# A decay table built from a tile already loaded, and a small load issued later

## The chip, the cores and the metric

One core of a Trainium2 chip. The metric is the device time of one execution in microseconds; the kernel before takes 591.12 us (median of 3 runs, 590.98 to 591.58). Engines: TensorE (PE; PEld is its weight load), VectorE (DVE), ScalarE (ACT), GpSimd (POOL) and SyncE (SP). Each of SP and ACT can issue DMAs on a queue of its own: in this profile q1 carries what SP issues, q10 what ACT issues. The work of all queues is done by the core's 16 DMA engines.

## The reference

Three stages, all in float32. First a decayed linear attention over 2 batches, 8 heads, 768 positions and head size 64:

```
for each block b of 64 positions:
    intra = (q_b k_b^T * Dmask) v_b          # Dmask[h,i,j] = lam[h]^(i-j) for i >= j, else 0
    inter = (q_b * lam[h]^(i+1)) kv_state
    out_b = intra + inter
    kv_state = lam[h]^64 * kv_state + (k_b * lam[h]^(63-i))^T v_b
```

`lam` has 8 values, one per head. The result, as 1536 tokens of 512, goes through a gated feed-forward layer (`w_gate`, `w_val`, `w_out`, width 1536), and its result through a layer of 8 experts (width 1024): a router (`moe2_w_gate`, 512 x 8) picks one expert for each token, and the expert's output is scaled by the router's probability.

## The kernel before, in words

The attention works on 12 units: 6 chunks of 128 positions, 2 batches each, all 8 heads at once as 4 pairs. A unit loads three tiles `in0`, `in1`, `in2` (q, k, v) of 128 x 512; `load(u)` (line 227) issues them on SP, and five units are asked for at the start. Only unit 0's k is loaded in two halves. Then `em_T` (line 285) transposes q and k on PE (line 295), ACT copies the results (line 297), and POOL makes `kd`, the decayed k (line 304). `em_S` (line 307) computes the scores on PE (line 315) and DVE multiplies them by the table `dec` (line 318). `em_O` (line 325) multiplies kd by v for the state (line 332), the state by the decayed q from the second chunk on (line 343), and the masked scores by v (line 347); ACT and DVE split the result into a rounded part and a rest (lines 353 and 356), `x1`. DVE keeps the state (lines 361 and 363).

Each engine runs its instructions in the order in which the program emits them; waits between engines are set by the tiles they read and write. In the first units the order is: transposes of unit u+1, then `em_O` of u, then scores of u+1.

Two tables are built at the start. `dec` (powers of lam, lower triangle, line 260) comes from `lam_b`, which holds the 8 values of lam in each of the 128 partitions (one load on ACT's queue, line 238). `lrep` (line 269) holds, in partition x*64+d, pair p, position i, the power i+1 of lam of head 2p+x; it is a running product on DVE over a scratch tile `d2`, whose first half holds the factors and whose second half holds the start values. `lrep` is read for the decayed q (line 301) and for the decay of the state (line 335), both from the second chunk on. Its factors come from `lam_s`, where partitions 0 to 63 hold the even heads' values and 64 to 127 the odd heads': two loads on ACT's queue (line 240), each with 64 partitions x 4 values taken with a stride of two. The scratch tiles `d0`, `d1`, `d2` are three of the four buffers tagged `raw`.

`wr`, the router's weights, is loaded on ACT's queue at line 248 and first read by `parts3` at line 574, in the second pass (t = 1) of the gate stage.

After the attention, `em_GV` (line 445) multiplies x1 by the gate and value weights in 36 groups of 24 matmuls (`mm3`, line 204), each product as three matmuls of rounded parts and rests. Weights come through the `raw` ring on SP's queue (`pump_dma`, line 102); ACT rounds a piece (line 141, `bg_begin`) and DVE computes the rest (line 149, `bg`). Some of these steps already run in the attention's last units. The matmuls of the output weights, the routing and the experts follow.

Of the kernel before, what the change touches and what calls it, by code (L numbers as in the profile page):

```python
# [8 lines left out]
F32 = mybir.dt.float32  # L9
# [11 lines left out]
def decayed_attention_two_moes(  # L21
# [14 lines left out]
    nc = tc.nc  # L36
    B, H, S, D = q.shape
# [3 lines left out]
    P = 128  # L41
    NP = H // 2
# [17 lines left out]
    const = ctx.enter_context(tc.tile_pool(name="const", bufs=1))  # L60
# [41 lines left out]
    def pump_dma():  # L102
        n = at["dma"]
        if n < len(pieces):
            src = pieces[n][2]
            pool, tag = ring.pop(0)
            ring.append((pool, tag))
            r = pool.tile([P, 1024], U32, tag=tag, name=tag)
            dst = (r if src.dtype == U32 else r.bitcast(F32))[:, 0:src.shape[1] * src.shape[2]]
            nc.sync.dma_start(out=dst.rearrange("p (a b) -> p a b", a=src.shape[1]), in_=src)  # L110
            raws[n] = r
            at["dma"] = n + 1
# [9 lines left out]
    def bg_begin():  # L122

        i = at["split"]
        if i >= len(pieces):
            return
        key, j, _src = pieces[i]
        if key not in W and not free:
            return
        if not (wide and i < N1):  # L130
            if i in raws:
                fin.append(raws.pop(i).bitcast(F32)[:, 0:512 if i < N1 else 1024])
        if not fin:
            return
        if key not in W:
            slot_of[key] = pool, s = free.pop(0)
            W[key] = pool.tile([P, 2048], F32R, tag=f"w{s}", name=f"w{s}")
        x = fin.pop(0)
        w = W[key][:, j * 1024:(j + 1) * 1024] if i < N1 else W[key]
        n = w.shape[1] // 2  # L140
        nc.scalar.copy(out=w[:, 0:n], in_=x)  # L141
        lop.append((i, w[:, n:2 * n], x, w[:, 0:n].bitcast(F32)))
        at["split"] = i + 1

    def bg(stage):
        if stage == 0:
            if lop:
                _i, lo, x, hi = lop.pop()
                nc.vector.tensor_tensor(out=lo, in0=x, in1=hi, op=ALU.subtract)  # L149
                pump_dma()  # L150
            if mid and not fin:
                a, r = mid.pop()
                nc.vector.tensor_scalar(out=a, in0=a, scalar1=2.25, scalar2=None, op0=ALU.max)
                cur.append((a, r))
        elif stage == 1:
            if cur:
                a, r = cur[0]
                u = a.bitcast(U32)
                nc.vector.tensor_scalar(out=u, in0=u, scalar1=3, scalar2=None, op0=ALU.logical_shift_left)
                nc.vector.scalar_tensor_tensor(out=u, in0=r[:, :, 1], scalar=0x80000000, in1=u,  # L160
                                               op0=ALU.bitwise_and, op1=ALU.bitwise_or)
            i = at["abs"]
            if wide and i < N1 and not mid and i in raws:
                r = raws.pop(i).rearrange("p (f w) -> p f w", w=2)
                a = cvp.tile([P, 512], F32, tag="cv", name="cv")
                nc.scalar.activation(out=a, in_=r[:, :, 1].bitcast(F32), func=ACTF.Abs, scale=65536.0)
                mid.append((a, r))
                at["abs"] = i + 1
        else:
            if cur:  # L170
                a, r = cur.pop()
                u = a.bitcast(U32)
                nc.vector.scalar_tensor_tensor(out=u, in0=r[:, :, 0], scalar=29, in1=u,
                                               op0=ALU.logical_shift_right, op1=ALU.bitwise_or)
                fin.append(a)
# [34 lines left out]
    nc.vector.memset(warm, 0.0)  # L210
    nc.scalar.activation(out=warm, in_=warm, func=ACTF.Tanh)
    lam_b = const.tile([P, H], F32, name="lam_b")
    lam_s = const.tile([P, NP], F32, name="lam_s")
    wr = const.tile([P, KD, E], F32, name="wr")

    rp = ctx.enter_context(tc.tile_pool(name="rp", bufs=2))
# [10 lines left out]
    def load(u):  # L227
        c, b = units[u]
        for n, src in enumerate((q, k, v)):
            t = ap.tile([P, H, D], F32, tag=f"in{n}", name=f"in{n}", bufs=5)  # L230
            w = H // 2 if u == 0 and n == 1 else H
            for h in range(0, H, w):
                nc.sync.dma_start(out=t[:, h:h + w, :],
                                  in_=src[b, h:h + w, c * P:(c + 1) * P, :].rearrange("h s d -> s h d"))
            qkv[u, n] = t

    load(0)
    nc.scalar.dma_start(out=lam_b, in_=lam.unsqueeze(0).to_broadcast([P, H]))
    for x in range(2):
        nc.scalar.dma_start(  # L240
            out=lam_s[x * D:(x + 1) * D, :],
            in_=lam.rearrange("(p x) -> x p", x=2)[x:x + 1, :].to_broadcast([D, NP]),
        )
    load(1)
    load(2)
    load(3)
    load(4)
    nc.scalar.dma_start(out=wr, in_=w_router.rearrange("(k p) e -> p k e", p=P))


    dec = ap.tile([P, 2, NP, P], F32, name="dec")
# [5 lines left out]
    for x in range(2):  # L257
# [3 lines left out]
        out=dec.rearrange(flat), data0=d0.rearrange(flat), data1=d1.rearrange(flat),  # L261
        initial=0.0, op0=ALU.mult, op1=ALU.add,
    )
    d2 = rawp.tile([P, 2, NP, P], F32, tag="raw", name="raw")
    nc.vector.memset(d2[:, 1], 0.0)
    nc.vector.tensor_copy(out=d2[:, 1, :, 0:1], in_=lam_s.unsqueeze(2))
    nc.vector.tensor_copy(out=d2[:, 0], in_=lam_s.unsqueeze(2).to_broadcast([P, NP, P]))
    nc.vector.memset(d2[:, 0, :, 0:1], 0.0)
    nc.vector.tensor_tensor_scan(
        out=lrep.rearrange("j p i -> j (p i)"),  # L270
# [14 lines left out]
    def em_T(u):  # L285
        c, b = units[u]
        for n in range(2):
            pt = bank(cnt["t"] % 2).rearrange("p (a b) -> p a b", a=NP)
            cnt["t"] += 1
            t = ap.tile([P, NP, P], F32, tag=f"tT{n}", name=f"tT{n}", bufs=2)  # L290
            w = NP // 2 if u == 0 and n == 1 else NP
            for p in range(NP):
                if p == w:
                    pt = bank(7).rearrange("p (a b) -> p a b", a=NP)
                nc.tensor.transpose(pt[:, p, :], pair(qkv[u, n], p), ident)  # L295
                if p % w == w - 1:
                    nc.scalar.copy(out=t[:, p + 1 - w:p + 1, :], in_=pt[:, p + 1 - w:p + 1, :])
            (qT, kT)[n][u] = t
            if n == 0 and c > 0:
                qd[u] = ap.tile([P, NP, P], F32, tag="qd", name="qd", bufs=3)  # L300
                nc.vector.tensor_tensor(out=qd[u], in0=t, in1=lrep, op=ALU.mult)
        if c < NCH - 1:
            kd[u] = ap.tile([P, H, D], F32, tag="kd", name="kd", bufs=2)
            nc.gpsimd.tensor_tensor(out=kd[u].rearrange("s (p x) d -> s p x d", x=2),
                                    in0=qkv[u, 1].rearrange("s (p x) d -> s p x d", x=2), in1=rev, op=ALU.mult)

    def em_S(u, conv):
        pss = []
        for x in range(2):
            pss.append(bank(2 + cnt["s"] % 3).rearrange("p (a b) -> p a b", a=NP))  # L310
            cnt["s"] += 1
        for p in range(NP):
            for x in range(2):
                r = slice(x * D, (x + 1) * D)
                nc.tensor.matmul(pss[x][:, p, :], lhsT=kT[u][r, p, :], rhs=qT[u][r, p, :], start=True, stop=True)  # L315
        for x in range(2):
            t = ap.tile([P, NP, P], F32, tag=f"at{x}", name=f"at{x}", bufs=2)
            nc.vector.tensor_tensor(out=t, in0=pss[x], in1=dec[:, x], op=ALU.mult)
            att_w[u, x] = t
            if conv:  # L320
                bg(1 + x)
        qT.pop(u)
        kT.pop(u)
# [49 lines left out]
    for u in range(NU):  # L373
        conv = u >= 4 and u % 2 == 1
        if conv:
            bg_begin()
        if u < AHEAD:
            em_T(u + 1)
            em_O(u, conv)
            em_S(u + 1, conv)  # L380
        else:
            if u == AHEAD:
                em_T(u + 1)
            if u + 2 < NU:
                em_T(u + 2)
            if u + 1 < NU:
                em_S(u + 1, conv)
            elif conv:
                bg(1)
                bg(2)  # L390
            em_O(u, conv)
        if u + 5 < NU:
            load(u + 5)
        if u in (2, 4):
            pump_dma()
            pump_dma()
    att.close()


# [452 lines left out]
    for n in range(len(seq) + LAG):  # L852
        bg(0)
        bg_begin()
        if n < len(seq):
            e, f = seq[n]
# [11 lines left out]
        if n >= LAG:  # L868
            e, f = seq[n - LAG]
# [125 lines left out]
```

## Time and profile before

| | |
|---|---|
| median of the runs (range) | 591.12 us (590.98 to 591.58) |
| profiled execution | 590.82 us |
| its span, from first to last record | 589.0 us |
| busy: PE, DVE, ACT, POOL | 561.8, 392.5, 241.6, 102.9 us |
| chain that ended last | PE 77%; issue 10%; DMA 5%; DVE 4%; POOL 2%; ACT 1% |
| packets on q1, q10 | 78128, 2768 |
| mean granted clock of PE | 0.992 |

The page also cuts the span into 40 slices of 14.7 us, with the busy share of each in tenths, 9 being 90% or more, PEclk being the granted clock:

```profile
PE   4999999999999999999999999989999999999991
PEclk9999999999999999999999999999999999999996
DMA  7999132322220322220122176327697677660000
```

The first slice and the last are the ones in which PE is far from full. Times in all views count from the start of the span; what lies between the span and the time of the execution is 590.82 - 589.0 = 1.8 us.

### The profile page before, as it was taken

The numbers are of one execution on the slowest core, as the hardware profiler recorded it, in microseconds if no ns is written. First come the engines' busy times: TensorE is split into PE (matmuls) and PEld (weight loads), VectorE is DVE, ScalarE is ACT, GpSimd is POOL, SyncE is SP. The second block draws the span as 40 slices with busy tenths as digits, with TensorE's granted clock in tenths as the row PEclk, the third lists the DMA queues.
The fourth block names the chain that finished last, engine by engine and source line by source line (L and its number), as shares of the span: only waits on it lengthen the run. The fifth ranks groups of instructions, "written<-read, shape, count | busy, mean of one in ns | idle before, by whom it ended". The sixth has DMA issues, their size and how long they took to land.

```text
span 589.0 us, 8506 instructions
## 1 busy us (share of the span) xinstructions
PE 561.8 (95%) x3202; PEld 465.6 (79%) x3202; DVE 392.5 (67%) x778; ACT 241.6 (41%) x434; POOL 102.9 (17%) x102
## 2 busy tenths in 40 slices
PE   4999999999999999999999999989999999999991
PEld 3888888888888888888888888678888888888881
DVE  4577799888414888562586467886868887777530
ACT  2343244443332444300343333234767666666420
POOL 3325200000000000000000013313265245142001
PEclk9999999999999999999999999999999999999996
DMA  7999132322220322220122176327697677660000
GB/s 130 203 242 215 38 108 107 108 92 88 74 69 0 108 85 95 71 72 0 35 75 101 41 251 195 112 106 232 156 303 247 207 264 238 198 204 28 0 25 31
DMA packets 84011, 72.97 MB, mean 124 GB/s; under 512 B 43228, under 2 KB 69852, under 8 KB 83968
## 3 DMA queue, kind: packets, MB, share of 16 engines
q1 hardware_dynamic: 78128, 65.02, 37.1%
q0 software_dynamic: 3072, 7.35, 3.7%
q8 instruction: 26, 0.43, 0.3%
q10 hardware_dynamic: 2768, 0.03, 0.3%
q14 instruction: 17, 0.14, 0.1%
HBM read 66.09 MB, written 7.08 MB: 124 GB/s over the span
## 4 chain that ended last, share of the span: by engine, by line
PE 77%; issue 10%; DMA 5%; DVE 4%; POOL 2%; ACT 1%; SPq 0%; POOLq 0%; ACTq 0%; DVEq 0%
PE b L204 58%; PE b L629 6%; PE b L630 3%; DMA in<-in_q_dram 2%; PE b L347 2%; PE b L332 2%; PE b L315 1%; PE b L295 1%; PE b L343 1%; DMA gg<-gd,g_idx 1%; POOL out_dram L674 1%; POOL xg L594 1%; PE b L512 1%; DMA xg<-x2d,g_first 1%; DMA in<-in_k_dram 1%
## 5 line engine op out<-in xcount | busy, mean ns | idle before, releaser
L204 PE MATMUL b<-x,w 128*128 128x512 f32 x864 | 199.6, 394 | 0.0
L204 PEld LDWEIGHTS b<-x,w 128*128 128x128 f32 x864 | 162.7, 188 | 36.3 <-issue 0.2
L204 PE MATMUL b<-w,hT 128*128 128x512 f32 x432 | 105.0, 398 | 0.0
L204 PE MATMUL b<-w,h 128*128 128x512 f32 (+1 forms) x384 | 101.0, 398 | 0.0
L204 PEld LDWEIGHTS b<-w,hT 128*128 128x128 f32 x432 | 79.9, 188 | 18.2
L629 PE MATMUL b<-xT,w 128*128 128x480 f32 x224 | 77.0, 383 | 0.1
L204 PEld LDWEIGHTS b<-w,h 128*128 128x128 f32 (+1 forms) x384 | 65.1, 183 | 14.7 <-ACT h L636 0.4
L630 PE MATMUL b<-xT,w 128*128 128x240 f32 x224 | 61.3, 274 | 0.0
L464 ACT CAST hT<-th 128x512 fp32r<-128x512 f32 x36 | 22.4, 622 | 87.3 <-DVE th L462 87.3
L629 PEld LDWEIGHTS b<-xT,w 128*128 128x128 f32 x224 | 42.1, 188 | 9.0 <-DVE hs L634 1.1
L460 DVE SCALAR_TENSOR_TENSOR th<-th,b 128x512 f32<-128x512 f32 x36 | 24.8, 688 | 33.8 <-ACT th L459 33.8
L630 PEld LDWEIGHTS b<-xT,w 128*128 128x128 f32 x224 | 42.5, 190 | 2.3
L504 POOL TENSOR_TENSOR xt<-xr,xt 128x512 bf16<-128x512 f32 x12 | 14.0, 1163 | 173.5 <-ACT xt L503 173.5
L459 ACT ACTIVATE th<-b 128x512 f32<-128x512 f32 x36 | 21.5, 598 | 55.3 <-PE b L204 55.3
L674 POOL DMA_INDIRECT out_dram<-y,s_idx x16 | 27.1, 1696 | 92.8 <-ACT y L673 74.0
L637 DVE SCALAR_TENSOR_TENSOR h<-hs,h 128x240 fp32r<-128x240 f32 x56 | 22.9, 409 | 26.4 <-ACT h L636 26.4
L149 DVE TENSOR_TENSOR w<-acc,w 128x1024 fp32r<-128x1024 f32 x32 | 38.9, 1221 | 1.5 <-ACT w L141 1.5
L462 DVE SCALAR_TENSOR_TENSOR th<-th,b 128x512 f32<-128x512 f32 x36 | 24.7, 687 | 19.1 <-PE b L204 19.1
L636 ACT ACTIVATE h<-hs 128x240 fp32r<-128x240 f32 x56 | 22.7, 405 | 34.6 <-DVE hs L634 34.6
L149 DVE TENSOR_TENSOR w<-raw,w 128x1024 fp32r<-128x1024 f32 x28 | 34.3, 1228 | 3.7 <-ACT w L141 3.4
L141 ACT CAST w<-acc 128x1024 fp32r<-128x1024 f32 x32 | 33.1, 1045 | 2.8 <-DMA raw<-in_moe_w_dram 2.7
L634 DVE TENSOR_TENSOR hs<-b,hs 128x240 f32<-128x240 f32 x56 | 22.6, 404 | 17.1 <-ACT hs L633 16.9
(133 smaller groups left out, 676.4 us busy)
## 6 DMA issues: line engine op xcount, KB each, us to landing
acc<-in_moe_w_dram SPq DMA_DIRECT2D x32, 512.0 KB, 4.4
raw<-in_moe_w_dram SPq DMA_DIRECT2D x28, 512.0 KB, 4.5
raw<-in_moe_w_gate_dram SPq DMA_DIRECT2D x12, 512.0 KB, 3.5
raw<-in_moe_w_val_dram SPq DMA_DIRECT2D x12, 512.0 KB, 3.5
raw<-in_moe_w_out_dram SPq DMA_DIRECT2D x12, 512.0 KB, 3.2
in<-in_q_dram SPq DMA_DIRECT2D x12, 256.0 KB, 5.0
in<-in_v_dram SPq DMA_DIRECT2D x12, 256.0 KB, 5.2
x2d<-acc SPq DMA_DIRECT2D x12, 256.0 KB, 3.3
```

The lines of the kernel that those rows point to most:

```text
L141: nc.scalar.copy(out=w[:, 0:n], in_=x)
L149: nc.vector.tensor_tensor(out=lo, in0=x, in1=hi, op=ALU.subtract)
L204: nc.tensor.matmul(acc, lhsT=a[x], rhs=b[y], start=first and n == 0, stop=last and n == 2)
L460: nc.vector.scalar_tensor_tensor(out=th, in0=th, scalar=1.0, in1=pg, op0=ALU.add, op1=ALU.mult)
L462: nc.vector.scalar_tensor_tensor(out=th, in0=th, scalar=0.5, in1=pv, op0=ALU.mult, op1=ALU.mult)
L464: nc.scalar.copy(out=hh[:, 0], in_=th)
L629: nc.tensor.matmul(ph, lhsT=hi, rhs=xt[:, kk], start=kk == 0, stop=kk == KD - 1, skip_group_check=True)
L630: nc.tensor.matmul(ph[:, 0], lhsT=lo, rhs=xt[:, kk, 0], start=False, stop=kk == KD - 1, skip_group_check=True)
L634: nc.vector.tensor_tensor(out=hs, in0=ph[:, 0], in1=hs, op=ALU.add)
L636: nc.scalar.activation(out=hh[:, 0], in_=hs, func=ACTF.Relu)
L637: nc.vector.scalar_tensor_tensor(out=hh[:, 1], in0=hs, scalar=0.0, in1=hh[:, 0].bitcast(F32), op0=ALU.max, op1=ALU.subtract)
L674: put = nc.gpsimd.indirect_dma_start(out=out, out_offset=bass.IndirectOffsetOnAxis(ap=si[0:m], axis=0), in_=y[0:m], in_offset=None, bounds ...
```

## The change

Three edits. The tile `lam_s` and its two loads are gone. The factors and start values of `d2` are copied from `lam_b` instead, for each half of the partitions with the heads of that half: the start values on DVE as before (two copies of 64 x 4 instead of one of 128 x 4), the factors on POOL (two copies of 64 x 512, each value repeated over 128 positions) instead of one copy of 128 x 512 on DVE. The load of `wr` stays on ACT's queue, but is issued after the last unit of the attention instead of after `load(4)`.

```diff
     lam_b = const.tile([P, H], F32, name="lam_b")
-    lam_s = const.tile([P, NP], F32, name="lam_s")
     wr = const.tile([P, KD, E], F32, name="wr")
...
     load(0)
     nc.scalar.dma_start(out=lam_b, in_=lam.unsqueeze(0).to_broadcast([P, H]))
-    for x in range(2):
-        nc.scalar.dma_start(
-            out=lam_s[x * D:(x + 1) * D, :],
-            in_=lam.rearrange("(p x) -> x p", x=2)[x:x + 1, :].to_broadcast([D, NP]),
-        )
     load(1)
     load(2)
     load(3)
     load(4)
-    nc.scalar.dma_start(out=wr, in_=w_router.rearrange("(k p) e -> p k e", p=P))
...
     nc.vector.memset(d2[:, 1], 0.0)
-    nc.vector.tensor_copy(out=d2[:, 1, :, 0:1], in_=lam_s.unsqueeze(2))
-    nc.vector.tensor_copy(out=d2[:, 0], in_=lam_s.unsqueeze(2).to_broadcast([P, NP, P]))
+    for x in range(2):
+        r = slice(x * D, (x + 1) * D)
+        lam_x = lam_b[r, :].rearrange("j (p x) -> j x p", x=2)[:, x, :].unsqueeze(2)
+        nc.vector.tensor_copy(out=d2[r, 1, :, 0:1], in_=lam_x)
+        nc.gpsimd.tensor_copy(out=d2[r, 0], in_=lam_x.to_broadcast([D, NP, P]))
     nc.vector.memset(d2[:, 0, :, 0:1], 0.0)
...
         if u in (2, 4):
             pump_dma()
             pump_dma()
+    nc.scalar.dma_start(out=wr, in_=w_router.rearrange("(k p) e -> p k e", p=P))
     att.close()
```

## Rows read from the trace of the kernel before

**Rows 1.** Busy time by stretch: stretch, PE, PEld, DVE, ACT, POOL, clock, DMA, GB/s
```profile
74.00:589.00 515.00, 499.02 (x2562) 411.27 (x2561) 345.62 (x697) 218.21 (x392) 76.67 (x61) 0.99 0.36 118
```
**Rows 2.** Waits of PE from 0 to 74 us: total, times, longest
```profile
PE b L295 <- DMA in<-in_q_dram: 5.6, 2, 4.7
PE b L295 <- DMA in<-in_k_dram: 2.6, 1, 2.6
```
**Rows 3.** Timeline, PE: start us, duration, engine, line, operation [idle before, releaser]
```profile
4.66 1.51 PE L295 MATMUL b<-ident,in 128*128 128x128 f32 x6 [4.66 <-DMA in<-in_q_dram]
...
8.75 0.69 PE L295 MATMUL b<-ident,in 128*128 128x128 f32 x2 [2.58 <-DMA in<-in_k_dram]
...
9.37 2.08 PE L315 MATMUL b<-tT,tT 64*128 64x128 f32 x16
...
12.40 2.29 PE L295 MATMUL b<-ident,in 128*128 128x128 f32 x8 [0.95 <-DMA in<-in_q_dram]
...
14.48 1.92 PE L332 MATMUL b<-in,kd 128*128 128x128 f32 x8
...
16.33 1.39 PE L347 MATMUL b<-at,in 128*64 128x128 f32 x16
...
17.64 1.16 PE L315 MATMUL b<-tT,tT 64*128 64x128 f32 x16
```
**Rows 4.** DMA queues, 0 to 4 us: packets, MB, share of 16 engines
```profile
q1 hardware_dynamic: 1420, 0.36, 39.4%
```
**Rows 5.** DMA queues, 4 to 8.5 us
```profile
q1 hardware_dynamic: 881, 0.22, 21.6%
q10 hardware_dynamic: 474, 0.00, 4.8%
```
**Rows 6.** DMA queues, 8.5 to 10.2 us
```profile
q1 hardware_dynamic: 1339, 0.34, 90.0%
q10 hardware_dynamic: 552, 0.02, 18.0%
```
**Rows 7.** DMA queues, 10.5 to 14.5 us
```profile
q1 hardware_dynamic: 3439, 0.87, 125.1%
```
**Rows 8.** Timeline, DMA issues on ACT and SP
```profile
2.78 0.62 ACTq L248 DMA_DIRECT2D wr<-in_moe_w_gate_dram  x1
...
5.01 4.49 SPq L233 DMA_DIRECT2D in<-in_k_dram  x1
```
**Rows 9.** Timeline, POOL and DVE in the first 13 us
```profile
1.37 1.16 POOL L258 COPY raw<-ident 128x512 f32<-128x512 f32 x2
...
5.05 2.29 DVE L260 TENSOR_TENSOR_SCAN dec<-raw 128x1024 f32<-128x1024 f32 x1
...
8.88 1.06 POOL L304 TENSOR_TENSOR kd<-in,dec 128x512 f32<-128x512 f32 x1 [5.42 <-DMA in<-in_k_dram]
...
9.71 0.25 DVE L266 COPY raw<-lam_s 128x4 f32<-128x4 f32 x1 [1.83 <-DMA lam_s<-in_lam_dram]
9.87 0.41 DVE L267 COPY raw<-lam_s 128x512 f32<-128x512 f32 x1
...
11.60 1.26 DVE L318 TENSOR_TENSOR at<-b,dec 128x512 f32<-128x512 f32 x2
```
**Rows 10.** Line 160, 40 to 75 us: duration ns min/median/max, first and last start
```profile
L160 DVE SCALAR_TENSOR_TENSOR cv<-raw,cv x2: 691/1060/1429, 55.5 to 73.4; 128x512 uint32<-128x512 uint32 x2
```
**Rows 11.** Timeline where the attention ends
```profile
73.85 0.59 ACT L353 CAST x<-b 128x512 fp32r<-128x512 f32 x1 [0.95 <-PE b L347]
...
74.86 0.62 ACT L141 CAST w<-cv 128x512 fp32r<-128x512 f32 x1 [0.42 <-DVE cv L173]
...
75.54 0.69 DVE L149 TENSOR_TENSOR w<-cv,w 128x512 fp32r<-128x512 f32 x1
...
73.73 6.47 PE L204 MATMUL b<-x,w 128*128 128x512 f32 x27
```
**Rows 12.** DMA queues, 60 to 80 us
```profile
q1 hardware_dynamic: 1013, 1.00, 17.1%
```

## The prediction

> **What bounds the kernel now.** I read the engines' busy time by stretch first, then TensorE's waits, its timeline at the start, and the DMA queues in short windows. From 74 us on PE is busy for 499.02 of 515.00 us [rows 1]: a microsecond taken off another engine there is worth nothing unless PE stood for it, and a microsecond by which PE enters that stretch sooner is worth a microsecond at the end. So the question is when the attention ends. In the attention PE waits for few things that last: q tiles (5.6 us in two waits, the first of 4.7 being the start itself) and one k tile, 2.6 us [rows 2]. The timeline puts them in the first unit. Six transposes end at 6.17; two more wait for the second half of unit 0's k until 8.75; the scores follow at 9.37 to 11.45; unit 1's transposes wait for its q until 12.40; from there PE runs on nearly without a gap [rows 3]. PE stands for 8.75 - 6.17 = 2.58 us and 12.40 - 11.45 = 0.95 us, both times for a DMA.
>
> Why are these two tiles late? The windows of the DMA queues tell it. Each q, k or v tile is 1024 packets of 256 B on queue q1; half a k is 512. By 4.0 us q1 has moved 1420 packets [rows 4]. In the next 4.5 us it moves only 881, while q10, ScalarE's queue, moves 474 [rows 5]. Then it moves 1339 in 1.7 us although q10 moves 552 beside it [rows 6], and undisturbed 3439 in 4 us, 860 per us [rows 7]. So between 4.0 and 8.5 q1 crawls at 881 / 4.5 = 196 per us with work waiting: the issue of unit 1's k on SP stands for 4.49 us, 5.01 to 9.50 [rows 8]. What q10 does in that stretch is lam_s: its 512 packets of 4 B follow the 128 of lam_b, and the DVE instruction that waits for lam_s goes at 9.71 [rows 9]. The packets of wr, as small in number (512) but read from different places, are q10's in the window where q1 is back at 1339 / 1.7 = 788 per us. I read this as: the reads of the one 32 B line of lam come through at about 474 / 4.5 = 105 per us whatever the engines could do, and hold up what stands behind them; the reads of wr don't.
>
> **The change part by part.** The sum is made against the profiled execution, 590.82 us.
>
> *The two lam_s loads go* (512 packets). The slow stretch should then end with lam_b, which the data for q1 before 4.0 already contain. With 860 per us from 4.0 on, packet 2048 (end of unit 0's k) is through at 4.0 + 628/860 = 4.7, packet 4096 (unit 1's q) at 4.0 + 2676/860 = 7.1, packet 5120 (unit 1's k) at 8.3. A tile lands later than its count, since the 16 engines don't keep step: I add 1.6 us, an estimate from two landings: unit 0's k released PE at 8.75, and its packet 2048 was through at 4.0 + 628/196 = 7.2; unit 1's q did so at 12.40, and packet 4096 was through at 10.2 + (4096 - 3640)/860 = 10.7 [rows 3 to 7]. That gives landings at 6.3, 8.7 and 9.9. PE then goes: six transposes to 6.2; the other two almost at once, 0.5 us, to 6.8; scores 6.85 to 8.95 (2.08 us); unit 1's transposes at 8.95 instead of 12.40. **Shift 3.45 us**, the 2.58 and the 0.95 less 0.1 for what is left of the first wait.
>
> It can be more or less, because PE's pace changes in this stretch: sixteen score matmuls take 2.08 us at 9.37 and 1.16 us at 17.64 [rows 3], a factor near that of the two clock levels (1.2 and 2.4 GHz), though the page's row of the granted clock has its highest digit in both slices. The step lies between 16.33 and 17.64. If it stays at that time, PE has 3.45 us more of slow work before it, worth 3.45 x 1.16/2.08 = 1.9 us: the low end. If it follows PE's own work, it comes earlier, since PE no longer stands still twice: unit 1's transposes are then bound by its k (9.9, done by 10.4), the eight L332 matmuls take about 1.1 us, and L347 starts at about 11.4 instead of 16.33: 4.9 us, the high end. I take 4.2, midway between the shift at today's pace and the high end.
>
> *What is late next.* L347 of unit 0 needs the masked scores of DVE line 318. DVE is free at 9.71 - 1.83 = 7.88 where it now waits for lam_s. From L266 to line 318 it takes 11.60 - 9.71 = 1.89 us now [rows 9]; the full-tile copy (0.41) moves to POOL and one more tiny copy comes (0.16, the step between L266 and L267), so line 318 starts at 7.88 + 1.64 = 9.52 and ends 1.26 later at 10.8. That is under 11.4, so it hides even in the high case, by 0.6 us.
>
> *Two copies of 64 x 512 on POOL.* Not in the trace in that form (a broadcast innermost). Bounds: 0 if wholly hidden; the nearest rows are POOL's copy of 128 x 512, 1.16/2 = 0.58, and its two-input instruction, 1.06 [rows 9]. I take 0.6 each, from lam_b's landing at about 4.1 to 5.3. DVE's second memset needs them at about 8.3; queued behind them on POOL are the two clears of the state (read only when unit 0 ends) and the decayed k (now at 8.88, then at about 7.4, since the table it needs ends at 5.05 + 2.29 = 7.34). At 1.06 each they end at 6.3: still hidden. Below nothing is excluded, since DVE loses only an instruction of 0.41.
>
> Against this speaks a row: DVE's L160 took 691 ns once and 1429 once, the latter with POOL at work beside it [rows 10]. If the two copies and the scan of 2.29 us exclude each other, either the scan ends 1.2 later or the copies run after it, 7.34 to 8.6, and line 318 ends at 11.1 to 11.9 and the decayed k at about 10.7. In the low and middle cases L347 comes later than that; in the high case it costs up to 0.5 us. The Trainium skill, "SBUF — State Buffer", section "SBUF: two separate sides", states it as a rule: the port pair that VectorE and GpSimd share is a lock held for a whole instruction, against two-input VectorE instructions too. By that rule the high end would be 4.4 us instead of 4.9; by the durations alone it stays.
>
> *wr's load moves to the end of the attention.* Its issue took 0.62 us on ScalarE at 2.78 [rows 8]; there it follows the last L353, 73.85 + 0.59 = 74.44 in today's times, and the DMAs of SP aren't behind it. Behind it on ScalarE is the cast L141 of the second piece of weights (74.86 now, after 0.42 us of idling), so it starts 0.2 us later; its correction on DVE (75.54, 0.69) then ends at 76.4. PE is at the first twelve matmuls of line 204 from 73.73, at (6.47 - 0.39)/26 = 0.234 us each, and wants the correction two matmuls after them, at 73.73 + 14 x 0.234 = 77.0 [rows 11]. Hidden, by 0.6 us: price nothing. The queues are near empty then (1013 packets from 60 to 80 us) [rows 12], so the issue should not stand as SP's did. Its own 552 packets at the front cost q1 little (788 against 860 per us over 1.7 us: 0.14 us), and wr is first read in the second of the three passes over the gate weights (line 574).
>
> Sum: 590.82 - 4.2 = 586.6. The median shown, 591.12, is 0.3 above the profiled time, so I forecast **586.9**; the cases from 1.9 to 4.9 give 589.2 to 586.2.
>
> **The rivals.**
>
> *The loads only stand in line.* If lam_s costs q1 no more than its packets' places, then 512 packets at 860 per us are 0.6 us and wr's another 0.6 at most: 590.5 to 589.9. For it: packets of q10 and q1 share the same engines, and from 4.0 to 8.5 q10 takes 4.8% of their time. Against it: in 4.0 to 8.5 both queues together moved 1355 packets in a time in which 3870 fit, so places were not what was short. The Trainium skill, "DMA: Bandwidth & Descriptors", section "Queues, rings and completion order", says that each engine goes round its queues packet by packet; taken alone that is this rival, and the trace disagrees by the 881 packets.
>
> *The slow stretch has another cause* (q1's own start, or lam_b, which stays). Then k and q land as now and only DVE's 1.8 us of waiting for lam_s goes, which is hidden: 591.1. For it: lam_b's reads go at the same pace. Against it: q1 is slow while lam_s is under way and no longer, and had moved 1420 by 4.0, lam_b's time.
>
> *Slower: wr's issue holds ScalarE.* If the issue at the end of the attention stands as the one on SP did, 4.49 us, the cast starts at 78.9 and the correction ends at 80.3, 3.3 us after PE wants it. With no gain at the start that is 594.4. It costs from an issue of about 1.2 us on, and turns the whole slower from where it exceeds the gain. For it: one row of 4.49. Against it: that one stood before a full queue.
>
> **How the numbers follow.** Forecast with all its cases 0.80, standing in line 0.08, another cause 0.08, slower 0.04. The range holds the first and reaches into the second, with 1 us below the high end's 586.2 for a pace or a start that comes sooner than I reckon: 585.2 to 590.2. What a measurement can tell from no change is about 0.2%, 1.2 us: faster 0.80, same 0.16, slower 0.04.
>
> **What would show it.** Right: q1 moves over 3000 packets between 4.0 and 8.5; the two waits of PE for k and q are under 0.5 us together; L347 starts between 11 and 13; line 204 starts near 69.5. Wrong: q1 still crawls to 8.5, or line 204 starts sooner but the end doesn't move with it, or PE shows a wait at the first weights. If L347 waits for DVE, the POOL copies are the step that failed.

## The result, and the profile after

The changed kernel takes 584.02 us (median; 583.75 to 585.81), the kernel before 591.35 in the runs beside it: a ratio of 0.988 with a 95% interval of 0.9856 to 0.9903. Forecast were 586.9 us and a range of 585.2 to 590.2. The direction was right, the gain was 7.3 us instead of 4.2, outside the range.

The profiled executions, 590.82 and 584.11 us with spans of 589.0 and 582.3, show where it went. Busy time by stretch, before and then after, cut where line 204 starts (columns as in [rows 1]):

```profile
0.00:73.73 73.73, 62.47 (x640) 54.06 (x640) 46.65 (x82) 23.26 (x42) 26.22 (x41) 1.00 0.78 165
73.73:589.00 515.27, 499.29 (x2564) 411.53 (x2562) 345.88 (x697) 218.35 (x392) 76.67 (x61) 0.99 0.36 118
```
```profile
0.00:69.50 69.50, 60.86 (x640) 52.65 (x640) 47.85 (x82) 23.23 (x42) 30.74 (x43) 1.00 0.87 175
69.50:582.30 512.80, 496.14 (x2564) 411.08 (x2562) 345.77 (x697) 218.79 (x392) 78.38 (x61) 0.99 0.37 119
```

The attention ends 4.2 us sooner, as forecast. But the rest of the kernel, the same instructions, is 515.27 - 512.80 = 2.5 us shorter too, and that nobody had asked for. Two groups of the page have it (line, operation, operands, count | busy us, mean ns | idle before), first before, then after:

```profile
L204 PE MATMUL b<-x,w 128*128 128x512 f32 x864 | 199.6, 394 | 0.0
L204 PE MATMUL b<-w,hT 128*128 128x512 f32 x432 | 105.0, 398 | 0.0
```
```profile
L204 PE MATMUL b<-x,w 128*128 128x512 f32 x864 | 198.4, 392 | 0.0
L204 PE MATMUL b<-w,hT 128*128 128x512 f32 x432 | 102.8, 394 | 0.0
```

The gate matmuls (x1 by w) lose 1.2 us in sum, the output matmuls (hT by w) 2.2; a wait of PE near 430 us, which the profiled execution of the kernel before doesn't have, gives 0.8 back. That wait belongs to the execution and not to the change: the kernel before has it too when it is profiled again, with 1.7 us. In the stretches of these matmuls nothing waits: they follow each other faster. By the starts of their records the output matmuls come every 233.3 ns before and every 227.0 in the mean after (226.7 but for a few longer gaps); the gate matmuls every 228.9 in both, except in the third of their three passes, 233.3 before and 228.9 after. Below, "gate sum" and "output sum" are these two numbers of a run's page.

The start, after the change. DMA queue q1 from 4 to 8.5 us, where [rows 5] had 881 packets:

```profile
q1 hardware_dynamic: 4082, 1.03, 124.5%
```

PE's waits up to 74 us (total, times, longest); the one of 2.6 us for k in [rows 2] is gone, and a new one for DVE has come:

```profile
PE b L291 <- DMA in<-in_q_dram: 4.8, 1, 4.8
...
PE b L343 <- DVE at L314: 0.7, 2, 0.5
```

And the timeline of PE, then of POOL and DVE, with the lines that answer to [rows 3] and [rows 9] (lines 291, 311, 328, 343 are 295, 315, 332, 347 of before; 314 is 318):

```profile
4.79 1.94 PE L291 MATMUL b<-ident,in 128*128 128x128 f32 x8 [4.79 <-DMA in<-in_q_dram]
6.83 2.08 PE L311 MATMUL b<-tT,tT 64*128 64x128 f32 x16
8.84 1.39 PE L291 MATMUL b<-ident,in 128*128 128x128 f32 x8
10.11 1.16 PE L328 MATMUL b<-in,kd 128*128 128x128 f32 x8
11.78 0.43 PE L343 MATMUL b<-at,in 128*64 128x128 f32 x2 [0.50 <-DVE at L314]
12.37 1.09 PE L343 MATMUL b<-at,in 128*64 128x128 f32 x14 [0.16 <-DVE at L314]
```
```profile
4.19 3.69 POOL L263 COPY raw<-lam_b 64x512 f32<-64x512 f32 x2 [1.66 <-DMA lam_b<-in_lam_dram]
...
8.04 1.08 DVE L262 COPY raw<-lam_b 64x4 f32<-64x4 f32 x2
...
9.00 2.99 POOL L300 TENSOR_TENSOR kd<-in,dec 128x512 f32<-128x512 f32 x2
...
9.29 1.85 DVE L265 TENSOR_TENSOR_SCAN lrep<-raw 128x512 f32<-128x512 f32 x1
...
11.06 1.26 DVE L314 TENSOR_TENSOR at<-b,dec 128x512 f32<-128x512 f32 x2
```

Scores start at 6.83, unit 1's transposes at 8.84, where 6.85 and 8.95 were reckoned. L343 then waits for the masked scores twice: DVE was expected to have them by 10.8 and has them by 12.3.

### The profile page after: what moved, and what is told of

Its sections match the earlier page's. It is cut to its first block, busy times and chain, and to the rows that moved or that the text cites. A ratio compares the mean times of both kernels' runs of the same rounds, so it can differ in the third digit from the quotient of the medians.

```text
span 582.3 us, 8504 instructions
## 1 busy us (share of the span) xinstructions
PE 557.0 (96%) x3202; PEld 463.7 (80%) x3202; DVE 393.6 (68%) x778; ACT 242.0 (42%) x434; POOL 109.1 (19%) x104
## 4 chain that ended last, share of the span: by engine, by line
PE 78%; issue 8%; DVE 7%; ACT 2%; DMA 2%; POOL 1%; SPq 0%; ACTq 0%; POOLq 0%; DVEq 0%
PE b L204 59%; PE b L626 6%; PE b L627 3%; PE b L343 2%; PE b L311 2%; DVE w L149 1%; PE b L328 1%; PE b L652 1%; PE b L339 1%; PE b L291 1%; POOL out_dram L671 1%; PE b L509 1%; DMA xg<-x2d,g_first 1%; DMA in<-in_k_dram 1%; ACT w L141 1%
## 5 line engine op out<-in xcount | busy, mean ns | idle before, releaser
L204 PE MATMUL b<-x,w 128*128 128x512 f32 x864 | 198.4, 392 | 0.0
L204 PE MATMUL b<-w,hT 128*128 128x512 f32 x432 | 102.8, 394 | 0.0
L141 ACT CAST w<-acc 128x1024 fp32r<-128x1024 f32 x32 | 33.2, 1045 | 2.8 <-DMA raw<-in_moe_w_dram 2.7
```

Of the source, the lines that this page charges most:

```text
L204: nc.tensor.matmul(acc, lhsT=a[x], rhs=b[y], start=first and n == 0, stop=last and n == 2)
```

## The experiments

Theories for the two parts: for the start, that the reads of lam hold q1 (against packets' places, size, or another cause); for the rest, that where tiles lie in the memory sets the pace of the matmuls. lam_s holds 16 bytes in each partition and takes 32, as the tiles are laid out; without it, x1, the weights and the raw ring lie 32 bytes lower in the compiled program, while hT on the other side stays. Rivals there: chance (the pace belongs to the execution) and timing (to what runs beside it).

**The two parts, apart.** The kernel before, again: no edit.

> The kernel before, unchanged, profiled a second time. In the first two traces the attention ends 4.22 us sooner after the change, and the other 2.5 us of the span come later: from 147 to 184 us and from 250 to 342 us the weight matmuls of line 204 follow each other every 233.3 ns before and every 226.7 or 228.9 ns after. If that pace belongs to the program (placement theory), it is here again: 233.3 in the output matmuls of the first pass, time 590.9 to 592.4. If it is a matter of the execution (chance theory), this trace may have another pace and the time moves by up to 2.5 us.

591.75 us, 0.9992 (0.9969 to 1.0015) of the kernel before in the runs beside it; sums 199.6 and 105.0, line 204 from 74.00. The pace repeats in a second profile: chance is out.

Then the changed kernel with lam_s's place left unused, and the kernel before with lam_s on the other side:

```diff
+    _hole = const.tile([P, NP], F32, name="hole")
     wr = const.tile([P, KD, E], F32, name="wr")
```


> The changed kernel with an unused tile of lam_s's size where lam_s lay, so that x1, the weights, the raw ring and everything else on that side of the memory lie 32 bytes higher again, as before the change. Placement theory: the attention still ends near 69.5 us, but the slow stretches come back (output matmuls of the first pass every 233.3 ns), time 586.5 to 587.2, 2.5 to 3 us over the changed kernel. Timing or chance theory: as the changed kernel, 583.7 to 585.8, pace 226.7.


```diff
-    lam_s = const.tile([P, NP], F32, name="lam_s")
...
+    lam_s = ap.tile([P, NP], F32, name="lam_s")
     for x in range(2):
```


> The kernel before with all its loads, but lam_s lies in the attention's own pool on the other side of the memory, so that x1, the weights and the raw ring lie 32 bytes lower, as in the changed kernel; the attention's q tiles move by 32 bytes. Placement theory: the start is as before (q1 crawls to 8.5 us, attention ends near 73.7), the later pace is that of the changed kernel (226.7), time 588.2 to 588.9. Timing or chance theory: 590.9 to 592.4.

With the gap: 587.88 us, 0.9928 (0.9898 to 0.9959), line 204 from 69.48, and the old sums to the digit. With lam_s moved: 590.68 us, 0.9959 (0.9935 to 0.9984), line 204 from 73.86, q1 951 packets from 4 to 8.5 us, and the new sums. Page of the first, then of the second:

```profile
L204 PE MATMUL b<-x,w 128*128 128x512 f32 x864 | 199.6, 393 | 0.0
L204 PE MATMUL b<-w,hT 128*128 128x512 f32 x432 | 105.0, 398 | 0.0
```
```profile
L204 PE MATMUL b<-x,w 128*128 128x512 f32 x864 | 198.4, 392 | 0.0
L204 PE MATMUL b<-w,hT 128*128 128x512 f32 x432 | 102.7, 393 | 0.0
```

Both times lie above the expected ones, as the kernel before does beside them (592.88 us); the ratios are what was expected. So each part goes with its own edit, and 0.9928 x 0.9959 = 0.989 is the whole. Timing is out: the second keeps the old start and has the new pace.

**wr's load.** The change with wr left at the front:

```diff
     load(4)
+    nc.scalar.dma_start(out=wr, in_=w_router.rearrange("(k p) e -> p k e", p=P))
...
-    nc.scalar.dma_start(out=wr, in_=w_router.rearrange("(k p) e -> p k e", p=P))
     att.close()
```


> The table from lam_b without the lam_s loads, the load of wr left at the front; addresses as in the changed kernel. If lam_s alone caused the crawl of q1 from 4.0 to 8.5 us, the attention ends within 0.3 us of the changed kernel (69.5), q1 moves over 3500 packets in that stretch and the time is 583.7 to 585.8. If wr's 512 packets at the front cost too, the end of the attention comes 0.5 to 1 us later and the time is 584.5 to 586.

584.84 us, 0.9883 (0.9828 to 0.9938), line 204 from 69.41 where the changed kernel has 69.50, q1 3910 packets. In the trace the moved load buys and costs nothing that can be seen; the interval of the times is too wide to tell less than 3 us.

**Why the reads of lam are slow.** lam_s differed from wr in two things: 4 B against 32 B, and one place against many. Two loads that nothing reads, put back into the changed kernel where lam_s was loaded, cross them:

```diff
+    dead = ap.tile([P, 4, H], F32, name="dead")
+    for x in range(2):
+        nc.scalar.dma_start(out=dead[:, 2 * x:2 * x + 2], in_=lam.unsqueeze(0).unsqueeze(0).to_broadcast([P, 2, H]))
```


> The changed kernel with two loads that nothing reads, where lam_s was loaded: 512 packets of 32 B, all from the 32 B of lam (lam_s: 512 packets of 4 B from the same bytes). If many reads of one place are slow, q1 moves about 900 packets from 4.0 to 8.5 us as before, PE waits 2 to 3 us for k, and the attention ends at 73 to 74 us. If the packets' size of 4 B was slow, q1 moves over 3500 and it ends near 69.5.


```diff
+    dead = ap.tile([P, 16], F32, name="dead")
+    for x in range(2):
+        nc.scalar.dma_start(
+            out=dead[x * D:(x + 1) * D, 0:NP],
+            in_=w_router[x * 256:(x + 1) * 256, :].rearrange("(p j) e -> p j e", j=NP)[:, :, 0],
+        )
```


> The changed kernel with two loads that nothing reads, where lam_s was loaded: 512 packets of 4 B, each from another row of the router's weights (32 B apart). If many reads of one place are slow, these are not: q1 over 3500 packets from 4.0 to 8.5 us, attention ends at 69.4 to 70. If packets of 4 B are slow, q1 about 900 and the attention ends at 73 to 74.

The queues from 4 to 8.5 us, first 32 B from one place, then 4 B from many:

```profile
q1 hardware_dynamic: 900, 0.22, 22.0%
q10 hardware_dynamic: 472, 0.01, 4.8%
```
```profile
q1 hardware_dynamic: 3877, 0.97, 124.3%
q10 hardware_dynamic: 469, 0.00, 5.9%
```

As many packets of q10 fall into both windows, and q1 crawls in the first alone; line 204 starts at 73.04 and 69.47 (589.72 and 584.82 us, one execution each). The pace of q10 differs as well: from 4 to 5 us it moves 104 packets beside 184 of q1 with the one place, and 367 beside 951 with many places, where all of them are through before 6. So it is the one place, not the size and not the number of the packets; whether any place read so often does this, or only that of lam, wasn't tried. The first window matches [rows 5] nearly packet for packet.

Such reads don't hold q1 from the start, though. From 2 to 4 us the kernel before has 172 packets on q10, lam_b's and the first of lam_s, at 86 per us; beside them q1 moves 1358, nearly as many as after the change (1381). Why the crawl begins only at 4.0 isn't shown.

**Which places set the pace.** Each matmul has a stationary operand (`lhsT`, which the weight load PEld brings in) and a moving one (`rhs`): the weights and x1 in the gate matmuls, hT and the weights in the output matmuls. Two theories to start with: the pace depends on whether the two begin alike modulo 64 bytes (both at even or both at odd multiples of 32), or on where the moving operand alone begins. Unused bytes move x1, the weights or hT.

The first edit meant for hT missed: the 32 bytes came to lie below the pool's other tiles and moved none of them, so that run is the changed kernel once more (198.4 and 102.7, line 204 from 69.53; 588.26 us in one execution, with a mean granted clock of 0.987 against 0.994).

> The changed kernel with 32 unused bytes ahead of hT, so that hT starts at an even multiple of 32 bytes while the weights and x1 stay at odd ones (before: hT odd, weights and x1 even; after: all odd). If the pace of the output matmuls (stationary hT, moving weights) depends on whether the two lie alike modulo 64 bytes, they follow each other every 233.3 ns again and the attention's end and the gate matmuls stay as they are; time about 2 us over the changed kernel. If only the place of the moving weights counts, they stay at 226.7 ns.


```diff
+    _pad = rp.tile([P, 8], F32, name="pad", bufs=1)
     xp_stack = ExitStack()
```


> The changed kernel with 32 unused bytes ahead of x1, so that x1 (moving operand of the gate matmuls) starts at an even multiple of 32 bytes and the weights (stationary) stay at an odd one. Alike-modulo-64 theory: gate matmuls every 233 ns in all three passes instead of 228.9, output matmuls stay at 226.7; some 3 to 4 us more. Moving-operand theory: only the third pass, 284 to 340 us, goes to 233.3, about 1.3 us more. If neither, 228.9 as in the changed kernel.

588.98 us in one execution; sums 202.2 and 102.7, as by the alike-modulo-64 theory. Then three more, from the same two lines of padding (the gap in const, 32 bytes ahead of x1) and one behind hT:

```diff
         hh = mp.tile([P, 2, TG], F32R, tag="hT", name="hT", bufs=13)
+        if fc == 0 and g == 0:
+            _low = mp.tile([P, 8], F32, name="low")
```


> The changed kernel with unused tiles that put the weights at an even multiple of 32 bytes (as before the change) and leave x1 and hT at odd ones. So far: output matmuls (stationary hT, moving weights) 233.3 ns with the weights even, 226.7 with them odd; gate matmuls (stationary weights, moving x1) 233.3 with x1 even and the weights odd, 228.9 with both odd, and with both even 228.9 in two passes and 233.3 in the third. Moving-operand theory: the output matmuls every 233.3, the gate matmuls 228.9 in all three passes. Alike-modulo-64 theory: both 233.3.

> The changed kernel with hT at an even multiple of 32 bytes, weights and x1 at odd ones (what the run called hT moved was meant to be). Moving-operand theory: nothing moves, output matmuls 226.7, gate 228.9, time as the changed kernel. Alike-modulo-64 theory: output matmuls 233.3, gate 228.9, time 2 us more.

> The changed kernel with x1, weights and hT all at even multiples of 32 bytes. Moving-operand theory: output matmuls 233.3 (moving weights even). Alike-modulo-64 theory: output matmuls 226.7. Gate matmuls as in the kernel before by either, 228.9 and in the third pass 233.3, if that third pass belongs to x1 and the weights being even; if it came of the output matmuls ahead of it, it follows them.

One execution each: 591.5, 587.29 and 587.61 us. The moving-operand theory falls with the first two (gate 202.2; output 104.9 with the moving weights odd). In the last one the output matmuls run at 228.9 ns, a third value that neither theory had, and alike modulo 64 isn't the whole of it. The run with the weights even and x1 odd takes as long as the kernel before beside it (591.5, one execution each), with an attention that is 4.2 us shorter. Its two sums are 2.5 us above those of before, so placement can eat more than half of the change; a stop of PE of another 2.5 us between 400 and 470 us is part of the rest.

Then 64 bytes and 192 bytes ahead of x1 (the same line with 16 and 48 instead of 8), the first beside the changed kernel again:

> The changed kernel with 64 unused bytes ahead of x1. Over all runs so far the pace goes with the distance of the two operands modulo 128 bytes: output matmuls 226.7 ns at 0 (weights and hT both 96), 228.9 at 64 (all even: 0 and 64), 233.3 at 32; gate matmuls only seen at 64 (228.9) and 32 (233.3). Here x1 and the weights both lie at 96, distance 0. Distance theory: the gate matmuls fall to 226.7 ns, their sum from 198.4 to 196.5 us, the output matmuls stay at 102.8, time 1.5 to 2 us under the changed kernel of the same chip. Theory that only odd or even multiples of 32 count: gate sum 198.4 and the same time.

> The changed kernel, unchanged, on the same chip as the run with 64 bytes ahead of x1, to compare the two. Attention ends at 69.5 us, gate matmuls 198.4 and output matmuls 102.8 us in sum, time 0.986 to 0.990 of the kernel before. If the pace were a matter of the execution and not of the program, this second trace would show other sums.

> The changed kernel with 192 unused bytes ahead of x1. The distance modulo 128 fell with 64 bytes (gate sum 201.9 us at distance 0). Over all runs the pace still goes with one function of the distance from the stationary to the moving operand modulo 256: 0 gives 226.7 ns, 32 gives 233.3, 64 gives 228.9, 96 and 128 give 233.3, for output and gate matmuls alike; here x1 lies at distance 0 from the weights. If it is that, the gate matmuls go to 226.7 ns, their sum to 196.5 us, output stays at 102.8, and the time is 1.5 to 2 us under the changed kernel's (0.984 to 0.988 of before). If the gate matmuls have 233.3 here too (sum 202), the rule is another one, and only the pairs tried are known.

With 64: 587.56 us, 0.994 (0.9926 to 0.9953), gate sum 201.9: the distance modulo 128 falls. The changed kernel beside it: 584.39 us, 0.989 (0.9872 to 0.9908), 198.4 and 102.8. With 192: 582.97 us, 0.9829 (0.9801 to 0.9857), and the page has

```profile
L204 PE MATMUL b<-x,w 128*128 128x512 f32 x864 | 196.5, 389 | 0.0
L204 PE MATMUL b<-w,hT 128*128 128x512 f32 x432 | 102.5, 393 | 0.0
```

just the gate sum that was expected. That is the fastest version here, by its median and ratio; its interval and the changed kernel's first one still touch (0.9857 and 0.9856). All placements tried, with the distance of the moving operand's first byte from the stationary one's in the compiled program, modulo 256:

| kernel | gate: x1 - w | gate sum | output: w - hT | output sum |
|---|---|---|---|---|
| before, and after with the gap | 64 | 199.6 | 32 | 105.0 |
| after, and before with lam_s moved | 64 | 198.4 | 0 | 102.7 to 102.8 |
| 32 bytes ahead of x1 | 96 | 202.2 | 0 | 102.7 |
| weights even, x1 odd | 96 | 202.2 | 32 | 104.9 |
| hT even | 64 | 199.6 | 32 | 104.9 |
| all even | 64 | 198.4 | 64 | 103.4 |
| 64 bytes ahead of x1 | 128 | 201.9 | 0 | 102.6 |
| 192 bytes ahead of x1 | 0 | 196.5 | 0 | 102.5 |

The runs that leave these tiles where the changed kernel has them repeat its sums, but for an output sum of 103.4 in the run with the 32 B reads: 27 of its output matmuls fall between 372 and 400 us, where its granted clock is 0.94.

**What is late next at the start.** The building of the table moved behind unit 0:

```diff
-    d2 = rawp.tile([P, 2, NP, P], F32, tag="raw", name="raw")
...
+    def build_lrep():
+        d2 = rawp.tile([P, 2, NP, P], F32, tag="raw", name="raw")
...
+        if u == 0:
+            build_lrep()
         if u + 5 < NU:
             load(u + 5)
```


> The changed kernel with the whole building of the state's decay table (the POOL copies, DVE's small copies and the scan) moved behind unit 0; nothing reads the table before unit 2. After the change the output matmuls of unit 0 (L343) wait 0.7 us for DVE's masked scores, which stand behind that building. If DVE is what is late there, line 314 starts at about 9.0 instead of 11.06, L343 at 11.3 instead of 11.78 and goes through without a wait, and the attention ends about 1.1 us sooner, near 68.4; time 582.6 to 583.6, about 1.3% under the kernel before. If the building only moves its cost to units 1 and 2, the attention ends at 69.5 as before and the time is that of the changed kernel, 583.7 to 585.8.

Its trace, POOL and PE:

```profile
10.44 1.27 POOL L264 COPY raw<-lam_b 64x512 f32<-64x512 f32 x2
```
```profile
10.95 1.09 PE L345 MATMUL b<-at,in 128*64 128x128 f32 x16
...
20.82 1.37 PE L330 MATMUL b<-in,kd 128*128 128x128 f32 x8 [2.08 <-DVE st L359]
21.99 1.92 PE L341 MATMUL b<-qd,st 128*128 128x128 f32 x8
```

The first part came: the matmuls of the masked scores run at 10.95 without a wait. But the building then stands before DVE's work of unit 1, PE waits 2.08 us at 20.82, and line 204 starts at 71.48, 2 us later than without this edit. In all 587.06 us, 0.987 (0.9848 to 0.9893), no different from the changed kernel: the 2 us of the profiled execution, the slowest of its six, don't show in the ratio, and why isn't known. DVE was late at unit 0, and put off the same work makes it late at unit 2.

## Why the prediction was right and wrong

*Reading of the start: right.* The crawl of q1 was lam_s, and ended with it; 4082 packets from 4 to 8.5 us where over 3000 were named. The rival by which the loads only stand in line is refuted by the crossed pair: 512 packets on q10 in both, 900 against 3877 on q1. The rule of the Trainium skill that stood for it ("DMA: Bandwidth & Descriptors", "Queues, rings and completion order": round the queues, packet by packet) may hold, but here the price of a packet is not its place in the round. The remark that q1 had moved 1420 packets in lam_b's time was evidence against lam_b as the cause, but also a sign that slow reads of lam alone don't make the crawl; that part of the reading stays open. The other cause and the slow issue of wr fell too: the issue took 0.38 us and ran while ACT was at its cast, so the next cast (L141) came after the same idle time as in [rows 11]:

```profile
69.63 0.58 ACT L349 CAST x<-b 128x512 fp32r<-128x512 f32 x1 [0.96 <-PE b L343]
69.64 0.38 ACTq L393 DMA_DIRECT2D wr<-in_moe_w_gate_dram  x1
...
70.65 0.62 ACT L141 CAST w<-cv 128x512 fp32r<-128x512 f32 x1 [0.43 <-DVE cv L173]
```

*The shift of 4.2: right in size, and partly by luck.* It was the middle between two cases; one of them came in full, and a term priced at nothing took most of the surplus back. PE's pace did change sooner, as in the high case: L328's eight matmuls take 1.16 us at 10.11, against 1.92 at 14.48 in [rows 3] (the granted clock reads 1.00 in both stretches, so that it is the clock isn't shown there). Behind them L343 could have started at 11.27 instead of 16.33, 5.1 us sooner; the high end was 4.9 (its own parts, 10.4 and 1.1, make 11.5 and 4.8). The POOL copies took most of the difference back. They were taken at 0.6 us each and bounded at 1.06; beside DVE they took 3.69 together, while the two alone, in the run with the table later, take 1.27. DVE's two tiny copies took 1.08 instead of 0.32 and its scan 1.85 instead of 1.2, beside POOL's next instructions. So line 314 ends at 12.3 instead of 10.8, and the second group of L343 starts at 12.37. The row of L160 [rows 10] was the right warning, and the "up to 0.5 us" drawn from it was too small: L343 lost 0.7 us in waits. By the sign that the prediction gave itself, L347 (now L343) waiting for DVE, the term of the POOL copies failed, though not the number it went into.

The Trainium skill's rule on the shared port pair ("SBUF — State Buffer", "SBUF: two separate sides") agrees in direction: both engines' instructions stretch here when they meet, POOL's copies from 0.61 us to 1.81 in the mean, and no run here shows which of them held what.

*The step that failed* is one in the first part: "a microsecond by which PE enters that stretch sooner is worth a microsecond at the end". It took the 515 us after the attention as fixed in length, and so the removal of a tile as free of effect on all other tiles. Their length depended on the placement: taking away 32 bytes brought the distance from hT to the weights from 32 to 0 modulo 256, and with it 2.2 us in the output matmuls, and 1.2 in the third pass of the gate matmuls. The kernel before with only lam_s moved has both gains with the old start, and the changed kernel with the gap has neither. With its range built from the start alone, the forecast could not hold that. No row of before showed it, but a view could have raised the question: in the kernel before, PE has 263 gate matmuls in the 60 us from 180 us and 259 in the 60 us from 279, busy throughout and with the granted clock at 1.00 in both, so that one form has two paces in one kernel. The output matmuls show the same between the two kernels (window, PE busy and matmuls, granted clock, DMA share, GB/s; first before, then after):

```profile
147.00:177.00 30.00, 30.00 (x130) 1.00 0.22 70
```
```profile
143.00:173.00 30.00, 30.00 (x134) 1.00 0.21 70
```

*Open.* Why the distance of the operands matters isn't shown; the table is a list of pairs tried with these tiles, and moving a pool moves its neighbours too. And the third pass of the gate matmuls is at 233.3 ns with a distance of 64 wherever the output matmuls ran at 233.3, and at 228.9 where they didn't, while the second pass is at 228.9 in both: the distance of x1 and the weights alone doesn't tell its pace, and what else does isn't shown. Of the wait of PE near 430 us (0.8 us after and 2.5 in its repetition, none before and 1.7 in its repetition) the cause wasn't followed up.

## What to carry to other kernels

Broadcasting a few bytes of HBM into many partitions by hundreds of tiny reads costs far more than its bytes: read such a line as few times as possible, and make the other layouts of it on chip. An edit that adds or drops a tile moves every tile behind it, so before an edit of this size is credited with a gain, run it once with the old addresses (an unused tile in the gap) and once the old kernel with the new ones. And when matmuls without any wait change their pace, try the distance between their operands: 192 unused bytes took the gate sum from 198.4 to 196.5 us.

## What the runs showed of the hardware

- 512 reads of one 32 B place came through at about 105 per us on q10, and q1 on the same engines fell to 200 packets per us beside them; 512 reads of 4 B from as many places left q1 at 3877 / 4.5 = 862. The crawl began at 4.0 us: from 2 to 4 us q1 moved 1358 packets beside 172 of q10, which came through at 86 per us.
- Matmuls of 128x512 float32 words came every 226.7, 228.9 or 233.3 ns, by where their two operands lay, with the granted clock at 1.00; in the third pass of the gate matmuls by something more.
- PE's granted clock fell after a standstill: in the run with the table later, after the wait of 2.08 us, the stretch from 21.8 to 25.4 us has a granted clock of 0.56, near the lower of the two levels (1.2 against 2.4 GHz), and eight matmuls of line 341 took 1.92 us at 21.99 instead of 1.06 at 28.80:

```profile
18.74:20.80 2.06, 0.00 (x1) 1.00 0.73 155
...
21.80:25.40 3.60, 3.60 (x27) 0.56 1.01 217
25.40:27.40 2.00, 2.00 (x26) 1.00 1.22 224
```
